# A linear-attention and token-mixer block in float32: kv by four token tiles, and the feature map folded into q's weights by half-array products

## The chip, the cores and the metric

The kernel runs on one core of a Trainium2 chip. Its five engines work side by side and meet through semaphores: TensorE (PE in the profile; PEld is its weight load), VectorE (DVE), ScalarE (ACT), GpSimdE (POOL) and SyncE (SP), which issues most of the DMAs. The metric is the device time of one execution in microseconds; the figure for a kernel is the median over several runs.

## The reference

The input x has 2048 tokens of 512 channels. It passes a layer norm, an attention without a softmax over tokens, a second layer norm (twice, since the mixer normalises its own input again), and a perceptron across the tokens.

```
qkv = layernorm(x) @ wqkv                     # 32 heads of 16
pq, pk = q @ w_phi[h], k @ w_phi[h]           # 16x16 per head
phi(p) = concat(softmax(p), softmax(-p))      # 32 features per head
kv = sum_s phi_k[s,:] v[s,:] ; z = sum_s phi_k[s,:]
o  = (phi_q @ kv) / (phi_q . z + 1e-6)
h  = x + o @ wo
u  = gelu(layernorm(layernorm(h))^T @ w1 + b1)  # over tokens, 2048 -> 1792
out = h + (u @ w2 + b2)^T                       # 1792 -> 2048
```

Everything is float32. The logits of q and k are linear in the normalised x, so w_phi can be multiplied into the columns of wqkv that make q and k.

## The kernel before, in words

A token tile is 128 tokens (16 of them), a chunk 128 of the 512 columns of q, k or v, which is eight heads. Large products are done as three products of float32r parts (`mm3`, L60: high with high, high with low, low with high), each a matmul of 128 stationary columns and 512 moving columns. Lines are those of the kernel before.

First stage, weights. For each chunk the transposed weights `WR[c]` (128 rows, 512 columns) are loaded and centred (`center`, L252). `fold` (L264) multiplies the q and k chunks with `ph`, a 128 by 128 matrix that has a head's w_phi in each 16 by 16 block of its diagonal and zeros elsewhere: four plain float32 products of 128 stationary and 128 moving columns into one psum bank. Each such product is two records in the profile. `hi_w` (ScalarE, L280) and `lo_w` (VectorE, L284) split the bank into the float32r parts `wqh` and `wql`. For q the banks are the two buffers of the tile `pu`, which q's projections use next.

Second stage, tokens (L399). For each tile k's logits are projected (`pk_ps`), shifted by VectorE, exponentiated by ScalarE into `PK[t]` and normalised by GpSimdE (`k_norm`, L191); v is projected (`pv`) and scaled by ScalarE into `VS[t]` (L186). `v_kv` (L387) projects a tile of v and, at every even tile, calls `kv` (L201) for the two tiles before. `kv` adds a tile's phi_k against v to the psum bank `kvp`: 16 float32 products of 32 stationary and 64 moving columns, which use a quarter of the array's columns each. A few tiles of q (`pu`) are projected in this loop too.

Third stage (L633): kvp is masked (`kvS`, L508), transposed and copied; phi_q is scaled and transposed (`tn`, L528), multiplied with kv (L546), with wo (`po`), and the residual and second norm are made, while the first mixer products (`fill`) run beside. The fourth stage is the rest of the mixer: `pu` products until 382 us and then `py` (L767).

The order of each engine's work up to L351 and from L419 on is written out by hand (`manual_schedule`). Between them, that is for the last fold calls and the token loop, a scheduler with a timeline of its own places the instructions, and it may move work across the border; the buffer counts (`bufs=`) of `PK`, `VS` and the psum tiles limit how far.

Of the kernel before, what the change touches and what calls it, by code (L numbers as in the profile page):

```python
# [9 lines left out]
F32 = mybir.dt.float32  # L10
F32R = mybir.dt.float32r
AF = mybir.ActivationFunctionType
# [5 lines left out]
P = 128  # L18
S, D, H, DH, F = 2048, 512, 32, 16, 1792
NT = S // P  # L20
KD = D // P
NF = F // P
NG = 8
NPR = 2 * NG
Q_AT = (4, 6, 8, 9, 11, 13)
V_NOT = (0, 1, 11)
# [7 lines left out]
def block_kernel(ctx: ExitStack, tc: tile.TileContext, x, xT, wT, phic, wo, w1, b1, w2, b2,  # L34
                 kvmask, ident_in, out):
    nc = tc.nc
# [31 lines left out]
    ps_q = ctx.enter_context(tc.tile_pool(name="ps_q", bufs=2, space=PSUM, side="right"))  # L68
# [17 lines left out]
    kk = a1.enter_context(tc.tile_pool(name="kk", bufs=2))  # L86
# [8 lines left out]
    X, XH, EQ, PK, VS, SQ, PS, W = {}, {}, {}, {}, {}, {}, {}, {}  # L95

    def load_x(t):
        raw = kk.tile([P, KD, P], F32, name="xraw", bufs=3)
        nc.sync.dma_start(raw, xT[t])
        return raw  # L100

    def load_h(t):
        XH[t] = kk.tile([P, D], F32, name="xh", bufs=3)
        nc.sync.dma_start(XH[t], x[t * P:(t + 1) * P, :])

    def split_x(t, raw):
        X[t] = big.tile([P, 2, KD, P], F32R, name="xs", tag="big")
        split(X[t][:, 0], X[t][:, 1], raw, nc.gpsimd)
# [57 lines left out]
    def run(*lists):  # L166
        for op in turns(*lists):
            op()

    def exps(t, e):  # L170
        nc.scalar.activation(e, e, AF.Exp, scale=r1[:, t:t + 1])
# [2 lines left out]
        return e.rearrange("p g (a d) -> p (g a) d", d=DH)  # L174

    def k_ops(t, o):
        PK[t] = kk.tile([P, NG, P], F32, name="pk", bufs=len(V_NOT) + 3)
        run(logit_ops(o, PK[t], False))

    def k_logits(t):  # L180
        k_ops(t, proj(t, wkh, wkl, ps_k, "pk_ps"))
        exps(t, PK[t])

    def v_out(t, o):
        VS[t] = kk.tile([P, D], F32, name="vs", bufs=4)
        nc.scalar.activation(VS[t], o, AF.Copy, scale=r1[:, t:t + 1])  # L186

    def v_proj(t):
        v_out(t, proj(t, wvh, wvl, ps_v, "pv"))
# [11 lines left out]
    def kv(t):  # L201

        for n in range(4):
            for c in range(4):
                g = n // 2 * 4 + c
                j = 2 * g + n % 2
                nc.tensor.matmul(kvp[32 * c:32 * c + 32, n, :], VS[t][:, 32 * j:32 * j + 32],  # L207
                                 PK[t][:, g, n % 2 * 64:n % 2 * 64 + 64], start=(t == 0 and n == 0),
                                 stop=(t == NT - 1), skip_group_check=True)
# [8 lines left out]
    with tc.tile_pool(name="prep", bufs=1) as prep:  # L218
        pc = prep.tile([P, 72], F32, name="pc")
        ph = prep.tile([P, 4, P], F32, name="ph")  # L220
        WR = {}

        def load_w(c):
            if c % 2 == 0:
                pair = big.tile([P, 2, D], F32, name="wraw2", tag="big")
                WR[c], WR[c + 1] = pair[:, 0], pair[:, 1]
            nc.sync.dma_start(WR[c], wT[c * P:(c + 1) * P, :])

        nc.scalar.dma_start(pc, phic)
        for c in range(4, 8):  # L230
            load_w(c)
        xr = {0: load_x(0), 1: load_x(1)}
        nc.sync.dma_start(ident, ident_in)
        for c in range(8, 12):
            load_w(c)
        xr[2] = load_x(2)
        load_h(0)
        load_h(1)
        xr[3] = load_x(3)
        for c in range(4):  # L240
            load_w(c)
        load_h(2)
        xr[4] = load_x(4)
        load_h(3)
        nc.sync.dma_start(mask, kvmask)
        nc.sync.dma_start(b1s, b1)
        nc.sync.dma_start(b2s, b2)

        FO = {}
        HL = {0: (wqh, wql), 1: (wkh, wkl), 2: (wvh, wvl)}  # L250

        def center(c, vector):  # L252

            mu = prep.tile([P, 1], F32, name="mu", bufs=3)
            if vector:
                nc.vector.reduce_sum(mu, WR[c], axis=AX.X)
                nc.vector.tensor_scalar_mul(mu, mu, -1.0 / D)
                nc.vector.tensor_scalar(WR[c], WR[c], mu, None, op0=ALU.add)
            else:
                junk = prep.tile([P, D], F32, name="junk")  # L260
                nc.scalar.activation(junk, WR[c], AF.Copy, scale=-1.0 / D, accum_out=mu)
                nc.scalar.activation(WR[c], WR[c], AF.Identity, bias=mu)

        def fold(c, pool, name):  # L264
            FO[c] = pool.tile([P, KD, P], F32, name=name, tag=name)
            for kt in range(KD):
                if c < 8:
                    nc.tensor.matmul(FO[c][:, kt, :], WR[c][:, kt * P:(kt + 1) * P], ph[:, c % 4, :],
                                     start=True, stop=True)
                else:  # L270
                    nc.tensor.transpose(FO[c][:, kt, :], WR[c][:, kt * P:(kt + 1) * P], ident)

        def parts(c):
            return [w[:, :, c % 4 * P:(c % 4 + 1) * P] for w in HL[c // 4]]

        def hi_w(c, vector=False):
            if vector:
                nc.vector.tensor_copy(parts(c)[0], FO[c])
            else:
                nc.scalar.activation(parts(c)[0], FO[c], AF.Copy)  # L280

        def lo_w(c):
            hi, lo = parts(c)
            nc.vector.tensor_sub(lo, FO[c], hi)  # L284

        warm = ps_k.tile([P, P], F32, name="pk_ps", tag="pk_ps")
        for _ in range(WARM):
            nc.tensor.matmul(warm, ones, ones, start=True, stop=True)
        with tc.manual_schedule(engines={ET.PE, ET.DVE, ET.Activation, ET.Pool}):

            nc.gpsimd.tensor_mul(ph.rearrange("p c (a f) -> p c a f", f=DH),
                                 pc[:, 0:64].rearrange("p (c f) -> p c f", f=DH).unsqueeze(2).to_broadcast([P, 4, 8, DH]),
                                 pc[:, 64:72].unsqueeze(1).unsqueeze(3).to_broadcast([P, 4, 8, DH]))
            center(4, True)
            center(5, False)
            fold(4, ps_q, "pu")
            center(6, True)
            fold(5, ps_q, "pu")
            center(7, False)
            fold(6, ps_v, "pv")  # L300
            fold(7, ps_v, "pv")
            hi_w(4, True)
            hi_w(5, True)
            hi_w(6)
            split_x(0, xr[0])
            hi_w(7)
            for c in range(4, 8):
                lo_w(c)
            split_x(1, xr[1])
            k0 = proj(0, wkh, wkl, ps_k, "pk_ps", True)  # L310
            center(8, True)
            for c in range(9, 12):
                center(c, False)
            k1 = proj(1, wkh, wkl, ps_k, "pk_ps")
            for c in range(8, 12):
                fold(c, *((ps_q, "pu"), (ps_v, "pv"))[c // 10])
            k_ops(0, k0)
            split_x(2, xr[2])
            k_ops(1, k1)
            stats_x(0)  # L320
            k2 = proj(2, wkh, wkl, ps_k, "pk_ps")
            for c in range(8, 12):
                hi_w(c)
            for c in range(8, 12):
                lo_w(c)
            stats_x(1)
            exps(0, PK[0])
            split_x(3, xr[3])
            split_x(4, xr[4])
            v0 = proj(0, wvh, wvl, ps_v, "pv")  # L330
            k_ops(2, k2)
            stats_x(2)
            k3 = proj(3, wkh, wkl, ps_k, "pk_ps")
            k_norm(0)
            center(0, True)
            v_out(0, v0)
            exps(1, PK[1])
            center(1, False)
            exps(2, PK[2])
            v1 = proj(1, wvh, wvl, ps_v, "pv")  # L340
            k_ops(3, k3)
            fold(0, ps_q, "pu")
            fold(1, ps_q, "pu")
            k_norm(1)
            center(2, False)
            v_out(1, v1)
            hi_w(0)
            hi_w(1)
            lo_w(0)
            lo_w(1)  # L350
            center(3, False)  # L351
        stats_x(3)
        exps(3, PK[3])
        for c in range(2, 4):
            fold(c, ps_q, "pu")
            hi_w(c)
            lo_w(c)

    q = {"mm": 0, "logits": 0, "exp": 0, "sum": 0}

# [26 lines left out]
    def v_kv():  # L387

        nonlocal v
        v_proj(v)  # L390
        if v % 2 == 0:
            kv(v - 2)
            kv(v - 1)
        v += 1

    v = 2
# [106 lines left out]
    run(q_logits(0))  # L503
    assert v == NT
    q_mm()
    kv(NT - 2)
    kv(NT - 1)
    nc.vector.tensor_mul(kvS, kvp, mask.unsqueeze(1).to_broadcast([P, 4, 64]))  # L508


# [267 lines left out]
    for n, (sp, p) in enumerate(STEPS):  # L778
        t = 2 * sp
# [93 lines left out]
```

## Time and profile before

| | |
|---|---|
| median of three runs | 530.71 us (530.67 to 531.04) |
| profiled execution | 530.51 us, span 528.7 us |
| TensorE busy | 521.9 us, 4000 records |
| VectorE, ScalarE, GpSimdE busy | 379.6, 272.7, 231.3 us |
| DMA | 55.86 MB, mean 106 GB/s |

The page gives busy time per engine, the chain of work that ended last, and groups of instructions by line. In rows of the timeline the first figure is the start in us from the span's start, the second how long the row lasts, and x the number of records merged in it; the pair `64*128` names the rows and columns of the array that a record uses. A matmul's record is longer than the slot it takes, since matmuls are pipelined, so slots are read from start to start. In rows by source line the three figures are shortest, median and longest duration in ns.

### The profile page before, as it was taken

Reading aid. Unit: us, or ns where it says so; the run is one execution under the profiler, and the core shown is the slowest. Engines: PE = TensorE matmul, PEld = TensorE weight load, DVE = VectorE, ACT = ScalarE, POOL = GpSimd, SP = SyncE. Lnnn points to the kernel's source line nnn. Section 1 sums busy time; section 2 is a strip of 40 time slices with the busy share of each in tenths; the row PEclk is TensorE's granted clock in tenths of the full one; section 3 lists DMA queues with packets and bytes.
Section 4 is the critical chain, followed back from the end, with each engine's and each line's share of the span. In section 5 each row is a group of like instructions: output and inputs, shape, how many; then the busy total and the mean of one; then the engine's idle time right before and its main releaser. Section 6 shows DMA issues by size and latency. Waiting matters only on the chain.

```text
span 528.7 us, 10143 instructions
## 1 busy us (share of the span) xinstructions
PE 521.9 (99%) x4000; PEld 445.5 (84%) x4000; DVE 379.6 (72%) x680; ACT 272.7 (52%) x460; POOL 231.3 (44%) x190
## 2 busy tenths in 40 slices
PE   8999999999999999999999999999999999999996
PEld 7888888887877777777788888888899999999996
DVE  6993999876899888863426424825668878887784
ACT  6998834525247777676657323526444243343340
POOL 2589699876999988994335000000001101101110
PEclk9999999999999999999999999999999999999999
DMA  8644310012303223333255333533014555535631
GB/s 308 192 129 119 87 35 21 1 49 93 102 1 100 72 97 114 121 121 120 81 183 156 104 98 98 165 115 81 20 41 113 141 146 145 131 125 121 160 75 47
DMA packets 45488, 55.86 MB, mean 106 GB/s; under 512 B 3968, under 2 KB 33024, under 8 KB 45440
## 3 DMA queue, kind: packets, MB, share of 16 engines
q1 hardware_dynamic: 43136, 51.38, 31.0%
q0 software_dynamic: 2016, 3.67, 5.1%
q8 instruction: 31, 0.51, 0.4%
q10 hardware_dynamic: 288, 0.17, 0.1%
q14 instruction: 17, 0.14, 0.1%
HBM read 46.81 MB, written 8.39 MB: 104 GB/s over the span
## 4 chain that ended last, share of the span: by engine, by line
PE 96%; DVE 2%; ACT 0%; issue 0%; DVEq 0%
PE py L767 26%; PE pu L62 13%; PE pu L63 12%; PE pu L64 12%; PE po L62 3%; PE pv L63 3%; PE pv L64 3%; PE pv L62 3%; PE po L63 3%; PE po L64 3%; PE pk_ps L62 2%; PE pk_ps L64 2%; PE pk_ps L63 2%; PE tn L546 2%; PE tn L528 2%; PE kvp L207 2%
## 5 line engine op out<-in xcount | busy, mean ns | idle before, releaser
L805 POOL DMA_DIRECT2D out<-ot x14 | 12.5, 998 | 211.7 <-DVE ot L803 211.7
L767 PE MATMUL py<-uf,whi 128*128 128x256 f32 x560 | 96.2, 283 | 0.0
L62 PE MATMUL pu<-hs,whi 128*128 128x512 f32 x224 | 88.0, 396 | 0.0
L57 ACT ACTIVATE whi<-wraw 128x1792 fp32r<-128x1792 f32 x28 | 47.7, 1704 | 77.9 <-PE py L767 67.2
L63 PE MATMUL pu<-hs,whi 128*128 128x512 f32 x224 | 87.5, 391 | 0.0
L64 PE MATMUL pu<-hs,wlo 128*128 128x512 f32 x224 | 87.0, 390 | 0.2 <-DVE wlo L599 0.2
L767 PEld LDWEIGHTS py<-uf,whi 128*128 128x128 f32 x560 | 83.3, 192 | 0.0
L599 DVE TENSOR_TENSOR wlo<-wraw,whi 128x512 fp32r<-128x512 f32 x56 | 45.5, 823 | 48.7 <-ACT whi L607 48.3
L767 PE MATMUL py<-uf,wlo 128*128 128x256 f32 x280 | 69.9, 283 | 0.0
L58 DVE TENSOR_TENSOR wlo<-wraw,whi 128x1792 fp32r<-128x1792 f32 x28 | 56.6, 2022 | 17.2 <-ACT whi L57 17.1
L607 ACT ACTIVATE whi<-wraw 128x512 fp32r<-128x512 f32 x56 | 34.4, 626 | 45.5 <-PE pu L63 41.4
L64 PEld LDWEIGHTS pu<-hs,wlo 128*128 128x128 f32 x224 | 42.1, 188 | 9.6 <-DVE wlo L599 0.6
L62 PEld LDWEIGHTS pu<-hs,whi 128*128 128x128 f32 x224 | 42.0, 188 | 9.4
L767 PEld LDWEIGHTS py<-uf,wlo 128*128 128x128 f32 x280 | 49.7, 192 | 0.0
L63 PEld LDWEIGHTS pu<-hs,whi 128*128 128x128 f32 x224 | 42.1, 188 | 8.3
L442 POOL TENSOR_TENSOR ez<-eq,zB 128x1024 f32<-128x1024 f32 x16 | 39.3, 2458 | 3.9 <-ACT zB L489 3.9
L767 PE MATMUL py<-un,whi 128*128 128x256 f32 x224 | 38.4, 283 | 0.0
L195 POOL TENSOR_TENSOR pk<-pk,sk 128x1024 f32<-128x1024 f32 x16 | 31.0, 1942 | 9.8 <-DVE sk L194 9.0
L767 PEld LDWEIGHTS py<-un,whi 128*128 128x128 f32 x224 | 33.2, 192 | 0.1
L530 ACT ACTIVATE pht<-tn 128x512 f32<-128x512 f32 x32 | 17.4, 596 | 29.5 <-PE tn L528 29.5
L460 POOL TENSOR_TENSOR eq<-eq,w 128x1024 f32<-128x1024 f32 x16 | 31.0, 1940 | 3.0 <-DVE w L457 3.0
L199 POOL TENSOR_TENSOR zacc<-zacc,pk 128x1024 f32<-128x1024 f32 x13 | 31.3, 2407 | 0.6
(165 smaller groups left out, 1176.0 us busy)
## 6 DMA issues: line engine op xcount, KB each, us to landing
wraw<-in_w SPq DMA_DIRECT2D x112, 256.0 KB, 2.9
xraw<-in_xT SPq DMA_DIRECT2D x16, 256.0 KB, 3.0
xh<-in_x SPq DMA_DIRECT2D x16, 256.0 KB, 2.7
h<-in_x SPq DMA_DIRECT2D x16, 256.0 KB, 3.6
out<-h SPq DMA_DIRECT2D x16, 256.0 KB, 2.0
out<-ot POOLq DMA_DIRECT2D x14, 256.0 KB, 4.8
wraw<-in_wT SPq DMA_DIRECT2D x12, 256.0 KB, 5.0
wo<-in_wo SPq DMA_DIRECT2D x4, 256.0 KB, 3.6
```

The source lines that it names most:

```text
L57: nc.scalar.activation(hi, src, AF.Copy)
L58: lo_engine.tensor_sub(lo, src, hi)
L62: nc.tensor.matmul(o, ah, bh, start=first, stop=False)
L63: nc.tensor.matmul(o, ah, bl, start=False, stop=False)
L64: nc.tensor.matmul(o, al, bh, start=False, stop=last)
L195: nc.gpsimd.tensor_mul(heads(PK[t]), heads(PK[t]), sk.unsqueeze(2).to_broadcast([P, 2 * H, DH]))
L199: nc.gpsimd.tensor_add(zacc, zacc, PK[t])
L442: nc.gpsimd.tensor_mul(EZ[t], EQ[t], zB)
L460: nc.gpsimd.tensor_mul(heads(EQ[t]), heads(EQ[t]), W[t].rearrange("p g c h -> p (g c h)").unsqueeze(2).to_broadcast([P, 2 * H, DH]))
L599: LO.append(nc.vector.tensor_sub(wl_, raw, wh_).ins)
L607: nc.scalar.activation(wh_, raw, AF.Copy)
L767: nc.tensor.matmul(o, a[x], b[:, y], start=start and i == 0, stop=stop and i == 2, skip_group_check=True)
```

## The change

Two things change. `kv` is called for four tiles at a time, at every fourth tile of v, and `PK` and `VS` get two more buffers each. For q, `fold` gives way to `fold_q`, which takes two chunks at once and uses that `ph` is zero outside its diagonal blocks: rows 0 to 63 of a chunk make only features 0 to 63, rows 64 to 127 only the others. Each product has 64 rows, 128 stationary and 64 moving columns; the lower and the upper rows alternate and write to different psum tiles, each of which holds one half of the features of both chunks. `q_part` splits one such tile into the high (ScalarE) and the low (VectorE) part, with blocks of 64 columns. k's weights are folded as before. Lines after the insertion move by up to 17.

```
     def k_ops(t, o):
-        PK[t] = kk.tile([P, NG, P], F32, name="pk", bufs=len(V_NOT) + 3)
+        PK[t] = kk.tile([P, NG, P], F32, name="pk", bufs=len(V_NOT) + 5)
...
-        VS[t] = kk.tile([P, D], F32, name="vs", bufs=4)
+        VS[t] = kk.tile([P, D], F32, name="vs", bufs=6)
...
+        def fold_q(c):
+            fo = [ps_q.tile([P, 2, KD, 64], F32, name="pu", tag="pu") for _ in range(2)]
+            for i in range(2):
+                for kt in range(KD):
+                    for r in range(2):
+                        f = slice(64 * r, 64 * r + 64)
+                        nc.tensor.matmul(fo[r][:, i, kt, :], WR[c + i][f, kt * P:(kt + 1) * P], ph[f, c + i, f],
+                                         start=True, stop=True, skip_group_check=True)
+            FQ[c] = fo
+
+        def q_part(c, r, lo):
+            fo = FQ[c]
+            hi_, lo_ = [w[:, :, c * P:(c + 2) * P].rearrange("p k (i r f) -> p r i k f", i=2, r=2)[:, r] for w in HL[0]]
+            if lo:
+                nc.vector.tensor_sub(lo_, fo[r], hi_)
+            else:
+                nc.scalar.activation(hi_, fo[r], AF.Copy)
...
-            fold(0, ps_q, "pu")
-            fold(1, ps_q, "pu")
+            fold_q(0)
...
-            hi_w(0)
-            hi_w(1)
-            lo_w(0)
-            lo_w(1)
+            for lo in range(2):
+                for r in range(2):
+                    q_part(0, r, lo)
...
-        for c in range(2, 4):
-            fold(c, ps_q, "pu")
-            hi_w(c)
-            lo_w(c)
+        fold_q(2)
+        for lo in range(2):
+            for r in range(2):
+                q_part(2, r, lo)
...
-        if v % 2 == 0:
-            kv(v - 2)
-            kv(v - 1)
+        if v % 4 == 0:
+            for t in range(v - 4, v):
+                kv(t)
...
-    kv(NT - 2)
-    kv(NT - 1)
+    for t in range(NT - 4, NT):
+        kv(t)
```

More of the change, by code (lines that the diff above doesn't have):

```diff
@@ L247, in block_kernel @@
         nc.sync.dma_start(b2s, b2)
-        FO = {}
+        FO, FQ = {}, {}
         HL = {0: (wqh, wql), 1: (wkh, wkl), 2: (wvh, wvl)}
```

## The prediction

> **What bounds the kernel now.** The page's busy table and its chain come first, then TensorE's list of waits, then the busy times of the long middle stretch.
>
> ```profile
> span 528.7 us, 10143 instructions
> PE 521.9 (99%) x4000; PEld 445.5 (84%) x4000; DVE 379.6 (72%) x680; ACT 272.7 (52%) x460; POOL 231.3 (44%) x190
> ...
> PE 96%; DVE 2%; ACT 0%; issue 0%; DVEq 0%
> ```
>
> ```profile
> PE pk_ps L288 <- DVE eps L53: 1.1, 1, 1.1
> PE pk_ps L124 <- ACT wkh L280: 0.8, 1, 0.8
> PE pu L64 <- DVE wlo L599: 0.2, 1, 0.2
> ```
>
> ```profile
> 40.00:520.00 480.00, 479.84 (x3714) 409.44 (x3713) 342.26 (x609) 236.71 (x385) 209.57 (x169) 1.00 0.35 98
> ```
>
> TensorE carries 96% of the chain, waits three times for other engines, and is busy 479.84 of 480 us from 40 to 520 at full clock. The row itself does not exclude short gaps (a matmul's record outlasts its slot), so I also compare starts. In the timeline the projections step evenly:
>
> ```profile
> 28.94 0.39 PE L62 MATMUL pk_ps<-wkh,xs 128*128 128x512 f32 x1
> ...
> 31.44 0.39 PE L64 MATMUL pk_ps<-wkh,xs 128*128 128x512 f32 x1
> 31.66 1.95 PE L268 MATMUL pu<-ph,wraw 128*128 128x128 f32 x16
> 33.37 0.48 PE L62 MATMUL pv<-wvh,xs 128*128 128x512 f32 x1
> 33.68 0.40 PE L63 MATMUL pv<-wvl,xs 128*128 128x512 f32 x1
> ```
>
> Eleven slots in 2.50 us: 0.227 us each. So the price of the change is what it does to TensorE's issue, slot by slot, as long as no wait appears; the other engines cost nothing while their slack lasts.
>
> **Part 1: kv by four tiles.** All 512 kv records stay (two per product); what changes is how often they interrupt the full-array matmuls.
>
> ```profile
> 53.03 0.39 PE L64 MATMUL pv<-wvh,xs 128*128 128x512 f32 x1
> 53.35 1.10 PE L207 MATMUL kvp<-pk,vs 128*32 128x64 f32 x64
> 54.38 0.19 PEld L62 LDWEIGHTS pu<-wqh,xs 128*128 128x128 f32 x1
> 54.49 0.19 PEld L63 LDWEIGHTS pu<-wql,xs 128*128 128x128 f32 x1
> 54.72 0.40 PE L63 MATMUL pu<-wql,xs 128*128 128x512 f32 x1
> ```
>
> The slot of the matmul at 53.03 ends at 53.26; that of the L62 after the burst begins at 54.72 - 0.227 = 54.49. The burst thus occupies 1.24 us. Inside it, narrower windows give the step:
>
> ```profile
> 53.50 0.90 PE L207 MATMUL kvp<-pk,vs 128*32 128x64 f32 x50
> 53.94 0.46 PE L207 MATMUL kvp<-pk,vs 128*32 128x64 f32 x19
> ```
>
> 50 - 19 = 31 records in 0.44 us: 14 ns each, 0.90 us for 64. The remaining 0.34 us is entry, exit and the first unhidden weight load: the fixed price of one burst. The chain has seven uncut bursts, of which these are the first and the last; the first pair is cut in two around eight fold records:
>
> ```profile
> 53.42 1.03 PE kvp L207 x64
> ...
> 141.55 1.03 PE kvp L207 x64
> ```
>
> ```profile
> 35.96 0.39 PE L64 MATMUL pv<-wvh,xs 128*128 128x512 f32 x1
> 36.27 0.64 PE L207 MATMUL kvp<-pk,vs 128*32 128x64 f32 x28
> 36.85 1.16 PE L268 MATMUL pu<-ph,wraw 128*128 128x128 f32 x8
> 37.93 0.75 PE L207 MATMUL kvp<-pk,vs 128*32 128x64 f32 x36
> 38.95 0.39 PE L63 MATMUL pk_ps<-wkl,xs 128*128 128x512 f32 x1
> ```
>
> The cut pair occupies (38.95 - 0.227) - (35.96 + 0.227) = 2.54 us; less 0.90 for kv and 0.90 for eight fold records (below), 0.74 is fixed price. The changed order has four bursts of 64 products, 128 records, none cut; the last still runs directly into the first transposes. Saved: 0.74 + 6 x 0.34 - 3 x 0.34 = **1.76 us**, last burst left out on both sides.
>
> **Part 2: the fold.** Before, the burst at 31.66 occupies (33.68 - 0.227) - 31.66 = 1.79 us for 16 records, 0.112 each; the two mode-equal borders cost nothing. 32 records: 3.58 us. After, each call is 16 products or 32 records, each with its own load of 128 stationary columns on 64 rows and 64 moving columns, the two halves alternating. The nearest row by shape is the transposes:
>
> ```profile
> 149.50 0.39 PE L64 MATMUL pu<-wqh,xs 128*128 128x512 f32 x1
> 149.81 0.57 PEld L528 LDWEIGHTS tn<-ident,eq 64*128 64x128 f32 x16 [0.35 <-issue]
> 150.45 0.50 PE L62 MATMUL pu<-wqh,xs 128*128 128x512 f32 x1
> 150.79 0.39 PE L63 MATMUL pu<-wql,xs 128*128 128x512 f32 x1
> ```
>
> They occupy (150.79 - 0.227) - (149.50 + 0.227) = 0.84 us; the 16 loads, each 0.138, end 0.57 after the first starts, so eight pairs step by (0.57 - 0.138) / 7 = 0.062 us, 0.50 in all, and the fixed price is 0.34 again. Two halves do run side by side. But these are transposes; the loads of ordinary products are longer:
>
> ```profile
> L268 PEld LDWEIGHTS pu<-ph,wraw x48: 186/192/323, 5.2 to 42.8; 128*128 128x128 f32 x48
> L207 PEld LDWEIGHTS kvp<-pk,vs x512: 106/110/110, 36.3 to 142.3; 128*32 128x32 f32 x171
> L546 PEld LDWEIGHTS tn<-pht,kvB x512: 102/107/108, 146.3 to 257.2; 64*32 64x32 f32 x171
> L528 PEld LDWEIGHTS tn<-ident,eq x256: 135/138/141, 142.5 to 253.7; 64*128 64x128 f32 x128
> ```
>
> From 32 to 128 columns a load grows by 82 ns, 0.85 ns a column, so 128 columns take 109 ns over a constant of 83; the same 0.11 stands between the two loads at 54.38 and 54.49, where nothing hid the first. Halving the rows (L207 against L546) saves 3 ns. A transpose's load is 138 - 83 = 55 ns, and its pair steps by 62, 7 more than the load. So I take for a pair of fold records 109 + 6 = **0.115 us**. Ends of the price: 0.062 (the transposes) and 0.22 (two loads one after the other). I take 0.115 because the load of a plain float32 product is nearest in kind, and the pairing in the transposes excludes nothing of its length. Two calls: 2 x (16 x 0.115 + 0.34) = 4.36 us, against 3.58: **+0.78 us**.
>
> The Trainium skill, "TensorE: Matmul & The Clock Gate", section "LDWEIGHTS (loading the stationary operand)", says that a load takes its columns over 1.2 GHz whatever the rows: 107 ns for 128. It speaks against this part: by it a pair is no cheaper than one old record, and the sum would move by 32 x 0.008 = 0.26 us down. The trace agrees on rows and on columns, except for the transposes' 55.
>
> **Edits at nothing, and their cover.** ScalarE and VectorE still make four high and four low parts of 512 elements each; runs of 64 instead of 128 could cost either sign, bounded by the 0.68 us of such a subtraction.
>
> ```profile
> L284 DVE TENSOR_TENSOR wql<-pu,wqh x4: 674/677/692, 35.7 to 43.9; 128x512 fp32r<-128x512 f32 x4
> 48.50 0.39 PE L62 MATMUL pu<-wqh,xs 128*128 128x512 f32 x1
> ```
>
> The last low part ends at 44.6, the first q product starts at 48.50: 3.9 us. The changed order puts one more pair of statistics ahead of the last high parts and makes both high parts wait for a whole call, so about 2 us of it stay. Both psum buffers are held until the low parts; q's product is queued behind that on TensorE, with k and v behind it. If the cover goes, each us late is a us lost. The second call waits for both low parts of the first; 30 matmuls, 6.8 us, lie between the two calls (12 before it until now), so no wait is expected there. kv of tile 7 still follows v of tile 8, as before, so no new releaser appears; older tiles only wait longer in two more buffers each (no DMA moves: SP's order and POOL's wait chain are the same but for early statistics). From the first transpose on TensorE's order is unchanged. The last burst doubles by 0.90 us, ahead of VectorE's mask; the 0.90 has left an earlier place, so it is neutral.
>
> **Sum.** -1.76 + 0.78 = -0.98 us. On the profiled execution, 530.51 us (span 528.7): 529.5; on the median of the runs, 530.71, which lies 0.20 above it: **529.7 us**, -0.18%.
>
> **Rivals.**
> - *The fold's loads hide, pairs step like the transposes.* For: equal shape and pairing. Against: 192 against 138 ns per load. Price: 2 x (16 x 0.062 + 0.34) = 2.66, -0.92 against before, total -2.68: 528.0 us. The Trainium skill, "TensorEngine Tiling (Array Packing)", section "Theoretical Speedup", promises up to 2x at 64 rows; no plain float32 product of this shape is in the trace.
> - *The two halves' loads go one after the other* (slower). Place: both fold calls. 32 x 0.22 + 0.68 = 7.72, +4.14, total +2.4: 533.1 us. It decides from 0.146 us a pair on. Against: sixteen transposes' loads fit in 0.57 us, pairwise.
> - *q's weights late* (slower): PSUM kept until the low parts, first q product waits. It decides once the slip passes 2 us of slack plus 0.98; a slip of 4 us gives 530.71 - 0.98 + 2 = 531.7.
> - *The gain is absorbed.* VectorE is almost full from 60 to 100:
>
> ```profile
> 60.00:100.00 40.00, 40.00 (x295) 32.78 (x294) 39.95 (x65) 20.09 (x29) 36.90 (x22) 1.00 0.10 27
> ```
>
>  A TensorE that runs ahead could meet it: 530.7. Against: no wait is listed there.
>
> **How the numbers follow.** Forecast 0.62, hidden loads 0.18, serial loads 0.07, late weights 0.05, absorbed 0.08. The forecast's own range is 529.2 to 530.2: the step between 0.109 and 0.120 is +-0.2, and the stall of 0.2 at L599 may come or go. The 8-in-10 range, 527.9 to 530.8, adds hidden loads and absorption. I count 0.2%, 1.06 us, as about what a measurement can tell from no change; the forecast stands just inside, so a third of it (0.22) counts as faster with hidden loads: 0.40. Slower: 0.12. Same: 0.48.
>
> **What would show it.** kvp in four bursts of 128 records, each about 2.1 us to the next instruction, and no other TensorE gap until 127 us. The fold's 32 records from first start to next matmul in about 2.0 us (1.2: the hidden rival; over 3.5: the serial one), loads near 190 ns at 64*128. A q product waiting for ScalarE or VectorE near 48 us, or a new row in TensorE's waits, would make the forecast wrong.

## The result, and the profile after

The changed kernel takes 529.85 us (median of 19 runs, 529.19 to 531.25) against 530.78 us for the kernel before (19 runs, 530.29 to 531.24): ratio 0.9984, 95% interval 0.9977 to 0.9992. By the medians that is 0.93 us less, where 0.98 had been forecast; by the means, which the ratio compares here and below, it is 0.82.

The profiled execution of the changed kernel took 530.93 us, the second longest of its nineteen. Its page and its list of TensorE's waits say why:

```profile
span 528.9 us, 10200 instructions
PE 520.5 (98%) x4032; PEld 445.0 (84%) x4032; DVE 379.2 (72%) x680; ACT 272.7 (52%) x460; POOL 231.6 (44%) x190
...
PE 94%; DVE 3%; DMA 1%; ACT 0%; issue 0%; SPq 0%; DVEq 0%
```

```profile
PE pv L268 <- DVE wraw L258: 1.2, 1, 1.2
PE pk_ps L307 <- DVE eps L53: 1.1, 1, 1.1
PE pk_ps L124 <- ACT wkh L299: 0.8, 1, 0.8
PE pu L268 <- DVE wraw L258: 0.5, 1, 0.5
PE pu L64 <- DVE wlo L616: 0.2, 1, 0.2
```

The two L258 rows are waits for the centring of k's weights, in the first ten microseconds. This code is the same in both kernels, and the two rows are missing before. Behind the longer one stands a load: VectorE waited 1.88 us for a chunk of weights by DMA and began on it at 7.08 us, where it began at 5.04 before. None of the six experiments in the table below, which open with the same code, has this late start, so I put it down to the one execution and compare the profiles by stage. The table takes from each trace the start of the first k product (L124), the time from there to the first transposes of the third stage (L528 before, L545 after), from there to the first `py` product, and from there to the end. All times are in us; the rows below the second are experiments, told further down.

| profile | first k product at | to the transposes | to `py` | to the end |
|---|---|---|---|---|
| before | 10.06 | 132.45 | 240.23 | 145.97 |
| after | 11.38 | 131.27 | 240.30 | 145.95 |
| kv by four alone | 10.11 | 130.56 | 240.30 | 145.97 |
| fold by half rows alone | 9.99 | 134.90 | 240.29 | 145.93 |
| fold alone, not cut | 10.37 | 134.45 | 240.29 | 145.94 |
| fold with 64 stationary columns | 10.38 | 129.61 | 240.23 | 145.95 |
| fold with all rows | 9.93 | 134.20 | 240.26 | 145.94 |
| kv by one | 10.19 | 135.87 | 240.26 | 145.94 |

The stage to the transposes is the one that moves: the change saves 132.45 - 131.27 = 1.18 us there, the late start takes 1.32 back in this one execution, and 386.2 us after it do not move.

The fold, with its neighbours, in the timeline of the changed kernel, and its records by source line (shortest, median and longest in ns):

```profile
32.71 0.39 PE L64 MATMUL pk_ps<-wkh,xs 128*128 128x512 f32 x1
33.03 2.00 PE L280 MATMUL pu<-ph,wraw 64*128 64x64 f32 x32
34.96 0.50 PE L62 MATMUL pv<-wvh,xs 128*128 128x512 f32 x1
35.30 0.39 PE L63 MATMUL pv<-wvl,xs 128*128 128x512 f32 x1
```

```profile
L280 PEld LDWEIGHTS pu<-ph,wraw x64: 182/188/188, 33.0 to 43.7; 64*128 64x128 f32 x64
L280 PE MATMUL pu<-ph,wraw x64: 272/272/320, 33.0 to 43.7; 64*128 64x64 f32 x64
```

The call occupies (35.30 - 0.227) - (32.71 + 0.227) = 2.14 us, against 1.79 for the 16 records before. Its loads last 188 ns, like those of the full array, and not 138 like those of the transposes. Take off the fixed 0.34 of the forecast, and the sixteen pairs step by 0.112 us: just what a single record of 128 rows and 128 moving columns took.

The four bursts of kv in the chain (the rows between them are left out), and the first in the timeline:

```profile
53.75 1.92 PE kvp L207 x128
85.81 1.92 PE kvp L207 x128
117.88 1.93 PE kvp L207 x128
140.80 1.93 PE kvp L207 x128
```

```profile
53.36 0.39 PE L64 MATMUL pv<-wvh,xs 128*128 128x512 f32 x1
53.68 1.99 PE L207 MATMUL kvp<-pk,vs 128*32 128x64 f32 x128
55.60 0.50 PE L62 MATMUL pu<-wqh,xs 128*128 128x512 f32 x1
55.94 0.40 PE L63 MATMUL pu<-wql,xs 128*128 128x512 f32 x1
```

(55.94 - 0.227) - (53.36 + 0.227) = 2.13 us: 128 x 0.014 = 1.79 and 0.34 more, the same fixed price as a burst of half the length.

### The profile page after: what moved, and what is told of

The parts are those of the page before. It is cut to its first block, busy times and chain, and to the rows that moved or that the text cites. A ratio compares the mean times of both kernels' runs of the same rounds, so it can differ in the third digit from the quotient of the medians.

```text
span 528.9 us, 10200 instructions
## 1 busy us (share of the span) xinstructions
PE 520.5 (98%) x4032; PEld 445.0 (84%) x4032; DVE 379.2 (72%) x680; ACT 272.7 (52%) x460; POOL 231.6 (44%) x190
## 4 chain that ended last, share of the span: by engine, by line
PE 94%; DVE 3%; DMA 1%; ACT 0%; issue 0%; SPq 0%; DVEq 0%
PE py L784 26%; PE pu L62 13%; PE pu L63 12%; PE pu L64 12%; PE po L62 3%; PE pv L63 3%; PE pv L62 3%; PE pv L64 3%; PE po L63 3%; PE po L64 3%; PE pk_ps L62 2%; PE pk_ps L63 2%; PE pk_ps L64 2%; PE tn L563 2%; PE tn L545 2%; PE kvp L207 1%
## 5 line engine op out<-in xcount | busy, mean ns | idle before, releaser
L62 PE MATMUL pu<-hs,whi 128*128 128x512 f32 x224 | 88.0, 396 | 0.0
L57 ACT ACTIVATE whi<-wraw 128x1792 fp32r<-128x1792 f32 x28 | 47.7, 1704 | 77.9 <-PE py L784 62.2
L63 PE MATMUL pu<-hs,whi 128*128 128x512 f32 x224 | 87.5, 391 | 0.0
L62 PEld LDWEIGHTS pu<-hs,whi 128*128 128x128 f32 x224 | 42.0, 188 | 9.4
L63 PEld LDWEIGHTS pu<-hs,whi 128*128 128x128 f32 x224 | 42.0, 188 | 8.3
L195 POOL TENSOR_TENSOR pk<-pk,sk 128x1024 f32<-128x1024 f32 x16 | 31.0, 1944 | 8.0 <-DVE sk L194 8.0
```

What stands on the lines that cost most here:

```text
L57: nc.scalar.activation(hi, src, AF.Copy)
L62: nc.tensor.matmul(o, ah, bh, start=first, stop=False)
L63: nc.tensor.matmul(o, ah, bl, start=False, stop=False)
L195: nc.gpsimd.tensor_mul(heads(PK[t]), heads(PK[t]), sk.unsqueeze(2).to_broadcast([P, 2 * H, DH]))
```

## The experiments

Ratios are to the kernel before, run on the same chip in the same session; the two times in front of each are medians.

**kv by four alone** takes back the fold. The kv lines are those of the change, with an order that keeps a burst whole; `LAST` holds the products of v and q that were issued last:

```
+            with tc.issue_after(LAST[0]), tc.issue_after(LAST[1]):   # last v product, last q product
                 for t in range(v - 4, v):
                     kv(t)
```

> kv by four tiles as in the change, q's weights folded as before (eight products of 128 rows and 128 moving columns per pair of chunks); kv's products are also kept in issue order behind the last v and q products, so that no burst is cut. Burst theory (each burst that is dropped saves its fixed price): five prices go, 0.74 us for the cut pair and 3 x 0.34, together 1.76 us: ratio to before 0.9967, four bursts of 128 records with 0.34 us beyond 0.014 us a record. Rival (the gain is absorbed by VectorE or by buffers held longer): ratio 0.999 to 1.000 and a new row in TensorE's waits.

Measured: 528.72 us against 530.61, ratio 0.9961 (0.9947 to 0.9975). The stage to the transposes is 132.45 - 130.56 = 1.89 us shorter, against 1.76 expected, and TensorE's waits have no new row after the first ten microseconds. The rival falls: nothing absorbs what the bursts give up. The changed kernel, with the half-row fold added, is 131.27 - 130.56 = 0.71 us longer in that stage: the fold costs what two calls at 2.14 against 3.58 us make, 0.70.

**Fold by half rows alone** leaves kv at two tiles, with the buffers of before.

```
-        if v % 4 == 0:
-            for t in range(v - 4, v):
-                kv(t)
+        if v % 2 == 0:
+            kv(v - 2)
+            kv(v - 1)
```

> q's fold by half rows as in the change, kv by two tiles as before. In the built order the second fold call is now cut by the first kv pair into two pieces. Load theory: a fold call uncut takes 16 x 0.112 + 0.34 = 2.13 us against 1.79, so +0.69 us for two, and 0.2 to 0.8 us for the extra changes of mode: ratio 1.0017 to 1.0028. Rival (the half rows save time and the other part of the change lost it): ratio below 1.

Measured: 535.28 us against 530.61, ratio 1.0078 (1.0054 to 1.0102), with runs from 532.88 to 536.41. The sign was expected and the size was not. Its first profile, which happened to catch the shortest execution, shows 134.90 - 132.45 = 2.45 us more in the stage:

```profile
36.54 0.64 PE L207 MATMUL kvp<-pk,vs 128*32 128x64 f32 x28
38.10 1.10 PE L280 MATMUL pu<-ph,wraw 64*128 64x64 f32 x8 [0.92 <-DVE wql L288]
39.13 0.42 PE L207 MATMUL kvp<-pk,vs 128*32 128x64 f32 x14
39.49 2.00 PE L280 MATMUL pu<-ph,wraw 64*128 64x64 f32 x24
41.41 0.54 PE L207 MATMUL kvp<-pk,vs 128*32 128x64 f32 x22
```

The scheduler put the second call directly behind the first kv products. It is there before VectorE has emptied the two psum buffers, TensorE waits 0.92 us for the low part, and everything queued behind waits too. The prediction names this wait and sets 30 matmuls between the two calls against it; the order here does not have them. Without the wait, 1.53 us are left, the upper end of what was expected. The median lies another 2.4 us above this execution, which its profile cannot explain.

**The same kernel, profiled twice more.**

> The fold-only kernel once more, for a profile of one of its slower executions (its runs went from 532.9 to 536.4 us, and the one profiled was the fastest). Theory of the late weights: in a slower run TensorE's wait in front of the second fold call, 0.9 us in the first profile, is longer, up to 3 us or more. Rival: a wait of kv for GpSimdE's normalised tile, as in the uncut kernel, near 70 us.

> The same again, a second look at the spread: the same two theories with the same numbers.

Measured: 536.45 and 536.60 us, with 530.92 for the kernel before. Neither theory held: in both, the wait before the second call is 0.9 us as before, and there is no wait near 70 us. What differs is the clock. Windows of the first of the two (the column before DMA share and GB/s is the granted clock), and its timeline after the call:

```profile
39.00:40.00 1.00, 1.00 (x21) 0.84 (x21) 0.87 (x2) 1.00 (x4) 1.00 (x1) 0.99 0.00 0
40.00:41.00 1.00, 1.00 (x11) 1.00 (x10) 1.00 (x3) 1.00 (x3) 1.00 (x3) 0.50 0.00 0
...
45.00:46.00 1.00, 1.00 (x3) 0.79 (x3) 0.15 (x1) 0.97 (x4) 1.00 (x3) 0.50 0.47 94
46.00:47.00 1.00, 1.00 (x4) 0.79 (x3) 0.00 (x0) 0.94 (x5) 1.00 (x1) 0.60 0.44 168
47.00:48.00 1.00, 1.00 (x6) 0.81 (x5) 0.00 (x0) 0.72 (x2) 1.00 (x3) 1.00 0.73 178
```

```profile
39.65 3.40 PE L280 MATMUL pu<-ph,wraw 64*128 64x64 f32 x24
...
45.22 0.63 PE L62 MATMUL pk_ps<-wkh,xs 128*128 128x512 f32 x1
45.65 0.63 PE L63 MATMUL pk_ps<-wkl,xs 128*128 128x512 f32 x1
```

From 40.0 to about 46.8 us TensorE runs at half clock: full matmuls stand 0.43 us apart instead of 0.227. In the other of the two the same dip lies from 41.0 to about 47.8. In both the stage is 138.0 us long, 3.1 more than in the execution without the dip, which has the same wait and a clock of 1.00. The clocks recorded with the six runs above agree: the three longest (536.15 to 536.41 us) have a mean granted clock of 0.991 to 0.994, the three others (532.88 to 534.41) of 0.997 to 0.999. So the ratio of 1.0078 mixes executions with the dip and without.

**Fold alone, not cut.** The first kv pair is kept behind the second fold call.

```
+            with tc.issue_after(LAST[0]), tc.issue_after(LAST[1]):   # LAST[1]: last fold product, then last q product
                 kv(v - 2)
                 kv(v - 1)
```

> The fold by half rows alone again, kv by two tiles, but the first kv pair is kept in issue order behind the second fold call, so neither is cut. Theory (the excess of the previous fold-only kernel came from the second call being issued early, into its wait for the low parts, and from the cut): the two calls cost 0.69 us more than before, the cut pair of before (0.74) becomes one burst (0.34): +0.3 us, or some 0.2 less where the burst borders on the call; ratio 1.0000 to 1.0010, with a spread of the runs under 1.5 us. Rival (the half-row fold itself costs some 4 us, or makes q's weights late whatever the order): ratio 1.005 or more.

Measured: 532.99 us against 530.82, ratio 1.0038 (1.0024 to 1.0052), runs from 532.61 to 533.22. The spread is gone, as expected, and all five runs have a mean clock of 0.998 or more. So the dip came with the early second call and its wait or with the cuts; this run takes out both together and cannot part them. But 134.45 - 132.45 = 2.0 us are left where some 0.1 to 0.3 were expected, and the timeline has most of it in one place:

```profile
68.89 0.65 PE L209 MATMUL kvp<-pk,vs 128*32 128x64 f32 x32
70.95 0.65 PE L209 MATMUL kvp<-pk,vs 128*32 128x64 f32 x32 [1.41 <-POOL pk L197]
71.53 0.50 PE L64 MATMUL pu<-wqh,xs 128*128 128x512 f32 x1
```

The second tile of this pair waits 1.41 us for GpSimdE's normalised phi_k (L195 in the kernel before); GpSimdE itself had waited 1.97 us for VectorE's sums. In the kernel before, the same pair starts at 68.20 and its second tile was normalised just ahead of it:

```profile
65.69 1.93 POOL L195 TENSOR_TENSOR pk<-pk,sk 128x1024 f32<-128x1024 f32 x1 [0.70 <-DVE ve L116]
```

It ends at 67.6, 0.6 us before the pair starts and about 1.1 us before TensorE comes to its second tile. So kv by two tiles has a thin cover there, and another order upsets it. kv by four asks for that tile only with tile 7, at 85.7 us, and in its profile tile 7 is normalised by 78.7. The rest of the 2.0 us is nearly as expected. The halted pair occupies (71.87 - 0.227) - (68.57 + 0.227) = 2.85 us against 1.23, 1.62 more. The two calls with the pair that follows the second take 2.14 + 3.18 = 5.32 us, against 1.79 + 2.54 + 0.90 = 5.23 before: 0.09 more. About 0.3 us I cannot place.

**Fold with 64 stationary columns.** Each product is split once more, so that four quarters of the array work side by side; kv as in the change, its bursts kept whole by the two lines of kv by four alone.

```
-                        nc.tensor.matmul(fo[r][:, i, kt, :], WR[c + i][f, kt * P:(kt + 1) * P], ph[f, c + i, f], ...)
+                        for j in range(2):
+                            nc.tensor.matmul(fo[r][64 * j:64 * j + 64, i, kt, :],
+                                             WR[c + i][f, kt * P + 64 * j:kt * P + 64 * j + 64], ph[f, c + i, f], ...)
```

> The change with each fold product split again into two halves of the stationary columns: 64 rows, 64 stationary and 64 moving columns, four of them side by side, 32 products a call; kv uncut as in the change. Load theory (a product's price is the load of its stationary columns): the load halves to about 0.054 us, groups of four step by about 0.066, a call takes 16 x 0.066 + 0.34 = 1.40 us against 2.13 in the change: 1.5 us less than the changed kernel, ratio to before 0.995. Rival (the step of 0.112 comes from something else, such as the number of products or their psum writes): no faster than the changed kernel, ratio 0.998 or more.

Measured: 528.01 us against 530.61, ratio 0.9946 (0.9932 to 0.9961): the fastest of all. Its timeline and its loads:

```profile
31.73 0.39 PE L66 MATMUL pk_ps<-wkh,xs 128*128 128x512 f32 x1
32.05 1.16 PE L283 MATMUL pu<-ph,wraw 64*64 64x64 f32 x64
33.14 0.50 PE L64 MATMUL pv<-wvh,xs 128*128 128x512 f32 x1
33.48 0.39 PE L65 MATMUL pv<-wvl,xs 128*128 128x512 f32 x1
```

```profile
L283 PEld LDWEIGHTS pu<-ph,wraw x128: 129/135/135, 32.0 to 42.0; 64*64 64x64 f32 x128
```

Twice as many products take (33.48 - 0.227) - (31.73 + 0.227) = 1.30 us a call instead of 2.14. Less 0.34, sixteen groups of four step by 0.060. The stage is 131.27 - 129.61 = 1.66 us shorter than in the change, 1.5 expected. So the number of products is not the price. The split does two things at once, and the step of 0.060 for four needs both: a load lasts 135 ns instead of 188, and four loads run side by side instead of two.

**Fold with all rows.** 128 rows again, still 64 moving columns and 16 products a call.

```
-                        nc.tensor.matmul(fo[r][:, i, kt, :], WR[c + i][f, kt * P:(kt + 1) * P], ph[f, c + i, f],
+                        nc.tensor.matmul(fo[r][:, i, kt, :], WR[c + i][:, kt * P:(kt + 1) * P], ph[:, c + i, f],
...
```

> The change with all 128 rows in each fold product (the zeros of the block-diagonal matrix are multiplied too), still 64 moving columns, 16 products a call. Load theory: two loads can no longer run side by side, 32 records a call step by 0.112 us each although they stream half the columns: 3.58 us a call against 2.13 in the change, no price for a change of mode: 2.9 us more than the changed kernel, ratio to before 1.003 to 1.004. Rival (moving columns set the price, 0.056 us a record): 1.8 us a call, ratio 0.997.

Measured: 532.53 us against 530.61, ratio 1.0037 (1.0024 to 1.0050), and the stage 134.20 - 131.27 = 2.93 us longer than in the change, as expected.

```profile
31.50 3.68 PE L280 MATMUL pu<-ph,wraw 128*128 128x64 f32 x32
34.98 0.48 PE L62 MATMUL pv<-wvh,xs 128*128 128x512 f32 x1
35.30 0.39 PE L63 MATMUL pv<-wvl,xs 128*128 128x512 f32 x1
```

32 records in (35.30 - 0.227) - 31.50 = 3.57 us: 0.112 each with 64 moving columns, as with 128 in the kernel before. So the moving columns are not the price either; what is left, and what made the difference in the experiment above, is the stationary columns.

**kv by one.** The change with a burst for every tile (two tiles in the first).

```
-        if v % 4 == 0:
-            for t in range(v - 4, v):
-                kv(t)
+        with tc.issue_after(LAST[0]), tc.issue_after(LAST[1]):
+            if v == 2:
+                kv(0)
+            kv(v - 1)
```

> The change with kv called for one tile at a time (two at the first call), kept in issue order behind the last v product. The built order has 16 separate bursts on TensorE against 4 in the change, one of them bordering on a fold call. Burst theory: 12 more prices of 0.34 us, less some 0.2: 3.9 us more than the changed kernel, 2.9 us more than before: ratio 1.0055. Rival (the price is not per burst but belongs to the longer buffers or the place of the work): ratio within 1.002 of before.

Measured: 534.16 us against 530.82, ratio 1.0062 (1.0048 to 1.0076). The stage is 135.87 - 131.27 = 4.6 us longer than in the change, 3.9 expected. One of its bursts of a single tile:

```profile
71.67 0.39 PE L64 MATMUL pu<-wqh,xs 128*128 128x512 f32 x1
71.98 0.65 PE L209 MATMUL kvp<-pk,vs 128*32 128x64 f32 x32
72.57 0.50 PE L65 MATMUL pu<-wql,xs 128*128 128x512 f32 x1
72.91 0.40 PE L66 MATMUL pu<-wqh,xs 128*128 128x512 f32 x1
```

(72.91 - 0.227) - (71.67 + 0.227) = 0.79 us for 32 records of 0.45: the fixed price is 0.34 again. Of the other 0.7 us of the stage, 0.2 is a new row in the waits (a k product for VectorE); the rest I cannot place. The price goes with the number of bursts.

## Why the prediction was right, point by point

- *TensorE's issue is the time.* Right. The two stages behind kept their lengths within 0.1 us, and each experiment's gain or loss in the second stage came out at the end.
- *A burst has a fixed price of 0.34 us, 0.014 a record.* Right: bursts of 32, 64 and 128 records all have 0.34 us over their records. The term was 1.76 us. Burst by burst the timelines give (2.54 - 0.90) + 6 x 1.23 + 1.03 = 10.05 us before and 2.13 + 2.12 + 2.13 + 1.92 = 8.30 in kv by four alone: 1.75. The stage gave 1.89; the other 0.14 lies between the bursts and is not placed.
- *A pair of fold records steps by 0.115, because its loads take as long as for 128 rows.* Right as a mechanism, 3% high: 0.112. The term was +0.78 us and measures 2 x 2.14 - 3.58 = +0.70. The rival of hidden loads (0.062) and that of serial loads (0.22) both fall by the same row, 2.14 us a call. The quarter-array fold shows the cause from the other side, since only fewer stationary columns made it faster.
- *The sum.* Right: -1.75 + 0.70 = -1.05 us by the bursts and calls themselves, against -0.98. The stage is 1.18 us shorter, the medians say -0.93 and the means -0.82, with an interval of -1.2 to -0.4. That the medians came within 0.05 of the forecast is luck; single runs of the changed kernel lie up to 2 us apart.
- *The low parts have some 2 us left.* Right that a cover stays, but it is thinner than 2 us. By the forecast's own measure, from the end of the last low part (47.7 + 0.68) to the first q product (L62), it is 1.35 us; the first product that reads the low part (L63 of `pu`) comes 1.8 us after it.

```profile
L288 DVE TENSOR_TENSOR wql<-pu,wqh x4: 671/677/692, 38.8 to 47.7; 128x512 fp32r<-128x512 f32 x4
49.73 0.39 PE L62 MATMUL pu<-wqh,xs 128*128 128x512 f32 x1
49.96 0.39 PE L63 MATMUL pv<-wvl,xs 128*128 128x512 f32 x1
50.19 0.39 PE L63 MATMUL pu<-wql,xs 128*128 128x512 f32 x1
```

The rival of late weights did not come. The other cover, the 30 matmuls between the calls, held too; the fold-only kernels show what it is worth, since with the second call moved up by the scheduler the wait for the low parts cost 0.92 us at once, and half the clock came on top in two of three profiles.

- *"No new releaser appears, older tiles only wait longer."* Right for the change, but it left something out. kv by two tiles started 0.6 us behind the end of GpSimdE's normalising at 68 us. kv by four removes that exposure. The prediction had not priced this slack, and in the run of the fold alone, not cut, 1.41 of the 2.0 us lost stand at that place.
- *Absorbed by VectorE.* Fell: kv alone gave its whole term.

## What to carry to other kernels

Before halving the rows of a small product, ask what its slot consists of: here one record of a plain float32 product (a product is two) with 128 stationary columns takes 0.112 us, with 128 moving columns or 64, and two records of 64 rows side by side take the same 0.112. So two halves only break even, and leaving and re-entering the full array is a loss; the change without its fold was the faster one (528.72 us). Splitting the stationary columns as well is what pays. And where the full-array stream is interrupted by tiled products, count the interruptions: each cost 0.34 us here, for bursts of kv of any length, for the 64-row fold and for the transposes, so collecting them is worth buffers.

## What the runs showed of the hardware that was not expected

TensorE's clock fell to 0.50 for about 6.8 us (40.0 to 46.8) behind a wait of only 0.9 us, in two of three profiles of one program; the clocks of its other runs point to three more of five. It began some 2 us after the wait had ended (38.27 in the profile shown). In the 6 us from 36 to 42 TensorE was still 5.1 us busy, with tiled float32 products on both sides of the wait, and it was just as busy in the execution without the dip. The Trainium skill, "TensorE: Matmul & The Clock Gate", section "What's actually happening", puts the half clock behind an idle window of some 3.4 us and calls that window free-running. The two lengths agree (6.8 is two windows), and so does that the dip comes in some executions and not in others. The idle time does not agree: the wait ahead of the dip is less than a third of a window. Whether tiled products count as less activity than full ones is one way to read it; no run here tells that apart. The uncut fold, with a wait of 1.41 us at 69 us between kv products, kept its clock at 1.00 in its profile.
